# Block products of gate and value in two rounds of 15, with sums of weights and substitutions on GpSimd

## The chip, the cores and the metric

The kernel runs on one core of one Trainium2 chip. The metric is device time in microseconds of one execution; lower is better. TensorE is called PE here, VectorE DVE, ScalarE ACT, GpSimd POOL and SyncE SP, as in the profile.

## The reference

A delta-rule attention block is followed by a SwiGLU feed-forward block, all in float32:

```python
# q, k, v: (4, 8, 768, 48), beta: (4, 8, 768)
k_n = k / (norm(k, axis=-1) + 1e-06)
state = zeros((B, H, D, D))
for t in range(S):
    y[:, :, t] = einsum('bhd,bhde->bhe', q[:, :, t], state)
    v_old = einsum('bhde,bhd->bhe', state, k_n[:, :, t])
    state += beta[:, :, t] * einsum('bhd,bhe->bhde', k_n[:, :, t], v[:, :, t] - v_old)
x = y.transpose(0, 2, 1, 3).reshape(3072, 384)
g, val = x @ w_gate, x @ w_val            # (384, 1536) each
out = (g / (1 + exp(-g)) * val) @ w_out   # (1536, 384)
```

## The kernel before

The sequence is cut into 12 chunks of 64 positions, so a chunk has 256 tokens (4 batches of 64) and its x is 384 by 256: three blocks of 128 features by two blocks of 128 tokens. Two chunks form a group, and the recurrence inside a chunk is solved with a triangular inverse that is made per group.

**Attention work.** `products` turns and multiplies k and q of a chunk (`gram`). `invert(g)` makes the inverse of group g: transposes, a power on POOL (L826), scaling (`scale_m`), then `substitute`, 31 steps of two dependent DVE operations each (L593 a product into `tmp`, L599 an addition to `zb`), then transposes. `join` (for group 1 `join_late`) completes the inverse with small matmuls. `advance(c)` has four steps: the old values (L918, L927), the new ones (L957), the state and the outputs (L1025, L1013), and last the transposes of y (L1086) and the copy into the chunk's x (L1092). Group 0 is solved apart at the start.

**Feed-forward work.** Chunks 0 and 1 use plain products (`gate_val`, L1289, and `output`, L1316) while the weights arrive and are converted. From chunk 2 on (`FAST`), gate and value are made in `gate_val_fast`, three rounds per chunk. A round takes two pairs of output blocks and forms the 12 products of 3 feature blocks, 2 pairs and 2 token blocks with 11 (7 for a 2 by 2 by 2 part, 4 plain). Each of these products is `product4`: four matmuls of 128 by 128 with 128 columns (L1193), for two blocks of gate and two of value, into one PSUM bank. Sums of weight blocks are made once by DVE (`sum_of_w`, spread over `output(1, 1)` by `sums_at`), are kept in device memory (`kept`), and are loaded by SP before each use (L1220). Sums of x are four DVE operations per chunk (`sums_of_x`, L1357). ACT copies partial results between banks (L1206, L1246, L1249) and DVE adds them (L1360); ACT's Silu (L1223) and DVE's product (L1228) end each result. `output_fast` multiplies by `w_out` with 7 products for 8 (L1399), with DVE sums of h.

**Order.** All engines' queues are written out by hand in program order. Between products, `point(c)` issues one step of attention work for the next chunk and `fill(n)` hands out pieces of `invert` until about n us of DVE work are spent; a piece that yields `WAIT` ends the fill, so that work on POOL has time. `finish` issues what is left of the next chunk's steps. `load_late` issues postponed loads on SP.

Of the kernel before, what the change touches and what calls it, by code (L numbers as in the profile page):

```python
# [15 lines left out]
R = 32  # L16
# [4 lines left out]
def kernel(  # L21
# [42 lines left out]
    ffn_pool = ctx.enter_context(tc.tile_pool(name="ffn", bufs=2))  # L64
# [129 lines left out]
    wg_sb = const.tile([128, KT, DFF], FP32, name="wg_sb")  # L194
    wv_sb = const.tile([128, KT, DFF], FP32, name="wv_sb")
# [392 lines left out]
    def substitute(mb, zb):  # L588
        for j in range(R - 1):
            m = R - 1 - j  # L590
            tmp = work.tile([128, 256], FP32, name="tmp", bufs=1)
            t_v = tmp[:, 0 : (j + 1) * m].rearrange("p (k i) -> p k i", i=m)
            nc.vector.tensor_tensor(  # L593
                out=t_v,
                in0=zb[:, 0 : j + 1, j : j + 1].to_broadcast([128, j + 1, m]),
                in1=mb[:, j : j + 1, j + 1 : R].to_broadcast([128, j + 1, m]),
                op=ALU.mult,
            )
            nc.vector.tensor_tensor(  # L599
                out=zb[:, 0 : j + 1, j + 1 : R],  # L600
                in0=zb[:, 0 : j + 1, j + 1 : R],
                in1=t_v,
                op=ALU.add,
            )
            yield
# [86 lines left out]
    def first_scale(r_b):  # L692
        zb, b = first_of["zb"], beta_b[:, 0]
        nb = work.tile([128, R], FP32, name="nb", tag="nb_1", bufs=1)
# [10 lines left out]
    def first_substitution():  # L705

        zb, mb = pairs_of_blocks(first_of["zb"]), pairs_of_blocks(first_of["mb"])
        for j in range(B16 - 1):
            m = B16 - 1 - j
            shape = [128, 2, m, j + 1]  # L710
            tmp = work.tile([128, 256], FP32, name="tmp", bufs=1)
            t_v = tmp[:, 0 : 2 * (j + 1) * m].rearrange(
# [64 lines left out]
    def join_late(g, c, tags):  # L777
# [9 lines left out]
        for m in range(M):  # L787
# [5 lines left out]
        t2 = work.tile(  # L793
            [128, M, R], FP32, name="t2", tag="r" if g else "tmp", bufs=2 if g else 1
        )
# [19 lines left out]
    def invert(g):  # L815
# [26 lines left out]
        for j, _ in enumerate(substitute(mb, zb)):  # L842
            yield 1 if g == 1 else 0.4 + (j + 1) * (R - 1 - j) / 340
        if g == 1:
            yield from late_z(g, zb)
            return
        yield from turn(z_v[:, R:C], zb.rearrange("p k i -> p i k"))
# [58 lines left out]
    def advance(c):  # L906
# [169 lines left out]
        xts[c] = ffn_pool.tile([128, KT, TOK], FP32, name="x_ffn")  # L1076
# [38 lines left out]
    def w_s(n, c):  # L1115
        if n < 4:
            return units(hp[5 + n])
        return units(hp[10] if c == FAST else p_places[0][:, 0:512])

    def m5_of(c, r):  # L1120
        early = c == FAST and r == 0
        return units(hp[13] if early else p_places[0][:, 512:1024])

    kept = {
        (n, r): dram.tile([128, 4, 128], FP32, name=f"w_s{n}_{r}")
        for n in (1, 2, 4)
        for r in range(3)
    }
    x_t = const.tile([128, 3, 128], FP32, name="x_t")

    def w_pair(m, t, f):
        return (wg_sb, wv_sb)[m][:, t, 128 * f : 128 * f + 256].rearrange(
            "p (i n) -> p i n", i=2
        )

    made_in = {
        0: {1: hp[6], 2: hp[7], 4: hp[10]},
        1: {1: hp[1], 2: hp[2], 4: hp[0]},
        2: {1: hp[12], 2: hp[13], 4: hp[8]},
    }  # L1140

    def sum_of_w(n, r):

        f1, f2 = 2 * r, 2 * r + 6
        for m in range(2):
            s1, s2, s4 = (units(made_in[r][k])[:, 2 * m : 2 * m + 2] for k in (1, 2, 4))
            if n == 1:
                plus(s1, w_pair(m, 0, f2), w_pair(m, 1, f2))
            elif n == 2:
                minus(s2, s1, w_pair(m, 0, f1))  # L1150
            elif n == 4:
                minus(s4, w_pair(m, 1, f1), s2)
            else:
                minus(w_pair(m, 0, f2), w_pair(m, 0, f1), w_pair(m, 0, f2))
        if n != 3:
            nc.sync.dma_start(out=kept[n, r], in_=units(made_in[r][n]))

    sums_at = {
        2: [(1, 1), (2, 1), (4, 1)],
        4: [(1, 2), (2, 2), (4, 2)],  # L1160
        6: [(3, 1), (3, 2)],
        8: [(1, 0), (2, 0)],
        12: [(4, 0), (3, 0)],
    }

    def sums_of_w(f):
        for job in sums_at.pop(f, ()):
            sum_of_w(*job)

    def sums_of_x(c):  # L1170

        left, right = slice(0, 128), slice(128, 256)
        b1, b2 = xts[c][:, 0], xts[c][:, 1]
        minus(x_t[:, 0], b1[:, right], b1[:, left])
        minus(x_t[:, 1], b2[:, right], x_t[:, 0])
        minus(b1[:, right], b2[:, right], b1[:, right])
        minus(x_t[:, 2], b2[:, left], x_t[:, 1])
# [8 lines left out]
    ROUNDS = 3  # L1186

    p_x, p_w, p_y, p_v = (units(bank) for bank in ffn_banks)
    tok = slice(0, 128), slice(128, 256)

# [7 lines left out]
    def plain(t, f):  # L1198
        return lambda u: w_pair(u // 2, t, f)[:, u % 2]

    def summed_w(n, c):
        return lambda u: w_s(n, c)[:, u]

    def begin(c, r):
        product4(p_x, plain(0, 2 * r), xts[c][:, 0, tok[0]], True)
        nc.scalar.copy(p_y, p_x)  # L1206

    def clear(part):
        area = ffn_banks[2 + part][:, 0:DH]
        nc.scalar.copy(area, mask_q[:, 0:1].to_broadcast([128, DH]))  # L1210

    def gate_val_fast(c, r, fill):

        f1, f2 = 2 * r, 2 * r + 6
        x, m5 = xts[c], m5_of(c, r)

        def next_sums(n):
            to = c + (r == ROUNDS - 1)
            if to < NCH:
                nc.sync.dma_start(out=w_s(n, to), in_=kept[n, (r + 1) % ROUNDS])  # L1220

        def silu(p, n):
            nc.scalar.activation(  # L1223
                sil[:, n].rearrange("p (i n) -> p i n", i=2), p[:, 0:2], ACTF.Silu
            )

        def times(p, n, f, j):
            nc.vector.tensor_tensor(  # L1228
                out=h_of(c, f, j),
                in0=sil[:, n].rearrange("p (i n) -> p i n", i=2),  # L1230
                in1=p[:, 2:4],
                op=ALU.mult,
            )

        more = 1.5 if (c, r) <= (FAST + 1, 0) else 0

        def combo_and_fill(n):
            if c == FAST:
                combos.pop(0)()
                n -= 1.9  # L1240
            fill(n)

        for f in (f1, f2):
            new_h(c, f, f // 2)
        product4(p_w, summed_w(1, c), x_t[:, 0], True)
        nc.scalar.copy(m5, p_w)  # L1246
        next_sums(1)
        product4(p_y, summed_w(2, c), x_t[:, 1])
        nc.scalar.copy(p_v, p_y)  # L1249
        next_sums(2)  # L1250
        load_late()
        product4(p_x, plain(1, f1), x[:, 1, tok[0]])
        product4(p_x, plain(2, f1), x[:, 2, tok[0]])
        plus(p_y, p_y, m5)
        product4(p_v, plain(0, f2), x[:, 0, tok[1]])
        silu(p_x, 0)
        fill(1)
        times(p_x, 0, f1, 0)
        plus(p_w, p_v, m5)
        point_and_fill(c + 1, 3.4 + more, fill)  # L1260
        product4(p_y, summed_w(4, c), x[:, 1, tok[1]])
        next_sums(4)
        load_late()
        product4(p_y, plain(2, f1), x[:, 2, tok[1]])
        silu(p_y, 1)
        times(p_y, 1, f1, 1)
        product4(p_w, plain(2, f2), x[:, 2, tok[1]])
        silu(p_w, 0)
        times(p_w, 0, f2, 1)
        product4(p_v, plain(1, f2), x_t[:, 2])  # L1270
        product4(p_v, plain(2, f2), x[:, 2, tok[0]])
        silu(p_v, 1)
        sums_of_h(c, f2)
        times(p_v, 1, f2, 0)
        if r < ROUNDS - 1:
            begin(c, r + 1)
        else:
            clear(0)
        point_and_fill(c + 1, 5 + more, combo_and_fill)
# [28 lines left out]
    def output(c, bp, fill, between=()):  # L1308
        p_o = ps_ffn([128, DM], "p_o", bp)
        for f in range(FT):  # L1310
            if f in between:
                fill(2)
                point(2)
                if (c, bp) == (1, 1):
                    sums_of_w(f)
# [61 lines left out]
    def s_of(x, f):  # L1377

        t = hp[8 + f // 2].rearrange("p (x i n) -> p x i n", x=2, i=2)
        return t[:, x - 1]  # L1380

    def sums_of_h(c, f):
        f1 = f - FH
        nc.vector.tensor_tensor(
            out=s_of(1, f1), in0=h_of(c, f1, 1), in1=h_of(c, f, 1), op=ALU.add
        )
        minus(s_of(2, f1), s_of(1, f1), h_of(c, f1, 0))
        minus(h_of(c, f1, 1), h_of(c, f1, 0), h_of(c, f1, 1))

    def output_fast(c, fill):  # L1390

        p = {(1, part): ps_ffn([128, DH], "p_o", 2 + part) for part in range(2)}

        def product(x, part, a, b):
            begun = (x, part) in p
            if not begun:
                p[x, part] = ps_ffn([128, DH], "p_o", 2 * x + part)
# [16 lines left out]
        def product_2():  # L1414
            product(0, 1, lambda f: s_of(2, f), lambda f: w_t2[:, f])
# [9 lines left out]
        def product_5():  # L1425
            product(1, 1, lambda f: s_of(1, f), lambda f: w_t1[:, f])
# [373 lines left out]
```

## Time and profile before

| | |
|---|---|
| runs | 695.4, 698.79, 699.6 us; median 698.79 |
| span of the profiled execution | 694.1 us |
| PE, DVE, ACT, POOL busy | 680.5, 473.1, 259.8, 53.5 us |
| granted TensorE clock | 0.997 of full speed |
| first and last L1289 (plain gate and value) | 44.8 and 129.6 us |
| first and last L1316 (plain output) | 129.8 and 169.7 us |
| first and last L1193 (fast gate and value) | 172.1 and 676.1 us |

The profiled execution's own whole time is not listed beside its span; the span lies 1.3 us below the lowest of the runs and 4.7 us below their median. A float32 matmul of the program stands as two records in the trace. Line numbers such as L1193 are those of the kernel before; those of the changed kernel differ.

### The profile page before, as it was taken

What the parts mean: (1) busy time and instruction counts of PE and PEld (TensorE: products, weight loads), DVE (VectorE), ACT (ScalarE), POOL (GpSimd) and SP (SyncE); (2) the same over time, 40 slices, a digit from 0 to 9 for tenths busy, and PEclk for the clock granted to TensorE, in tenths of its full rate; (3) what the DMA queues carried; (4) which work ended last, traced back from release to release, by engine and by line L of the source; (5) the groups of instructions that cost most, each with busy time, mean ns of one, the idle gap of its engine ahead of it and who ended that gap; (6) DMA issues with size and microseconds to landing.
All of it is one profiled execution on the core that took longest, in us unless ns stands there. A gap on an engine that the chain in (4) does not pass through costs nothing.

```text
span 694.1 us, 25652 instructions
## 1 busy us (share of the span) xinstructions
PE 680.5 (98%) x11380; PEld 635.6 (92%) x11380; DVE 473.1 (68%) x1104; ACT 259.8 (37%) x549; POOL 53.5 (8%) x62
## 2 busy tenths in 40 slices
PE   8799999999999999999999999999999999999997
PEld 4688888757999999999999999999999999999997
DVE  6887779798899758896469786389844345333342
ACT  4674776214442532344233244242153142142230
POOL 5110031105000030000300002100000000000000
PEclk9999999999999999999999999999999999999999
DMA  9567924017550621564432363243241231221210
GB/s 136 148 167 180 275 69 161 1 34 174 133 109 16 117 79 40 103 116 84 94 72 70 73 135 70 56 108 70 55 108 48 58 83 46 55 63 46 69 47 23
DMA packets 143854, 62.31 MB, mean 90 GB/s; under 512 B 122976, under 2 KB 126048, under 8 KB 143744
## 3 DMA queue, kind: packets, MB, share of 16 engines
q1 hardware_dynamic: 141536, 60.19, 37.0%
q8 instruction: 89, 1.46, 0.9%
q10 hardware_dynamic: 2080, 0.39, 0.4%
q0 software_dynamic: 128, 0.10, 0.1%
q14 instruction: 21, 0.17, 0.1%
HBM read 53.58 MB, written 7.08 MB: 87 GB/s over the span
## 4 chain that ended last, share of the span: by engine, by line
PE 90%; DMA 4%; SPq 3%; ACT 1%; issue 1%; DVE 1%; POOL 0%; ACTq 0%; POOLq 0%; DVEq 0%
PE ffn L1193 43%; PE ffn L1399 20%; PE ffn L1289 8%; PE ffn L1316 4%; DMA h_f<-in_moe_w_val_dram 3%; PE p_px L957 2%; PE p_px L918 2%; PE p_py L1013 2%; SPq L140 1%; PE p_py L927 1%; PE p_py L521 1%; PE p_px L1025 1%; PE p_px L521 1%; SPq L186 1%; PE p_py L1086 1%; DMA wo_sb<-in_moe_w_gate_dram 1%
## 5 line engine op out<-in xcount | busy, mean ns | idle before, releaser
L1193 PE MATMUL ffn<-x_ffn,wg_sb 128*128 128x128 f32 x840 | 128.3, 275 | 0.3 <-ACT x_ffn L1092 0.2
L1193 PE MATMUL ffn<-x_ffn,wv_sb 128*128 128x128 f32 x840 | 128.1, 275 | 0.0
L1193 PEld LDWEIGHTS ffn<-x_ffn,wg_sb 128*128 128x128 f32 x840 | 111.1, 192 | 0.6 <-ACT ffn L1249 0.3
L1193 PEld LDWEIGHTS ffn<-x_ffn,wv_sb 128*128 128x128 f32 x840 | 110.7, 192 | 0.0
L1223 ACT ACTIVATE sil<-ffn 128x256 f32<-128x256 f32 x120 | 46.1, 384 | 131.8 <-PE ffn L1193 127.1
L1399 PE MATMUL ffn<-wo_sb,h_f 128*128 128x192 f32 x480 | 83.4, 327 | 0.0
L1228 DVE TENSOR_TENSOR h_f<-sil,ffn 128x256 f32<-128x256 f32 x120 | 49.5, 418 | 47.7 <-ACT sil L1223 45.2
L1399 PEld LDWEIGHTS ffn<-wo_sb,h_f 128*128 128x128 f32 x480 | 78.1, 190 | 0.4
L1360 DVE TENSOR_TENSOR ffn<-ffn,p_sb 128x512 f32<-128x512 f32 x58 | 40.4, 696 | 44.1 <-ACT ffn L1249 43.0
L1193 PE MATMUL ffn<-x_t,h_f 128*128 128x128 f32 x480 | 61.1, 280 | 0.0
L1193 PEld LDWEIGHTS ffn<-x_t,h_f 128*128 128x128 f32 x480 | 56.2, 191 | 1.4 <-ACT ffn L1206 0.2
L599 DVE TENSOR_TENSOR zb<-zb,tmp 128x31 f32<-128x31 f32 (+15 forms) x155 | 53.1, 342 | 5.3
L593 DVE TENSOR_TENSOR tmp<-zb,mb 128x31 f32<-128x31 f32 (+15 forms) x155 | 52.6, 339 | 4.0
L826 POOL TENSOR_TENSOR n_b<-mb,half 128x32 f32<-128x32 f32 x5 | 30.0, 6003 | 289.2 <-DVE mb L563 289.2
L1360 DVE TENSOR_TENSOR o_sb<-o_sb,ffn 128x192 f32<-128x192 f32 x49 | 17.2, 351 | 51.2 <-PE ffn L1399 49.1
L1206 ACT COPY ffn<-ffn 128x512 f32<-128x512 f32 x30 | 17.1, 571 | 63.5 <-PE ffn L1193 57.1
L1399 PE MATMUL ffn<-last_k,h_f 128*128 128x192 f32 x200 | 35.9, 327 | 0.0
L1289 PE MATMUL ffn<-x_ffn,wg_sb 128*128 128x256 f32 x144 | 34.4, 385 | 0.0
L1289 PE MATMUL ffn<-x_ffn,wv_sb 128*128 128x256 f32 x144 | 33.8, 382 | 0.0
L1399 PEld LDWEIGHTS ffn<-last_k,h_f 128*128 128x128 f32 x200 | 32.9, 190 | 0.0
L1289 PEld LDWEIGHTS ffn<-x_ffn,wg_sb 128*128 128x128 f32 x144 | 26.5, 190 | 4.3 <-DVE wg_sb L309 0.7
L1289 PEld LDWEIGHTS ffn<-x_ffn,wv_sb 128*128 128x128 f32 x144 | 27.0, 190 | 3.7
(302 smaller groups left out, 1064.3 us busy)
## 6 DMA issues: line engine op xcount, KB each, us to landing
h_f<-w_s SPq DMA_DIRECT2D x60, 256.0 KB, 2.9
p_sb<-w_s SPq DMA_DIRECT2D x27, 256.0 KB, 2.7
vin<-in_v_dram SPq DMA_DIRECT2D x48, 96.0 KB, 3.2
out_dram<-o_sb SPq DMA_DIRECT2D x48, 96.0 KB, 2.2
kn<-in_k_dram SPq DMA_DIRECT2D x20, 192.0 KB, 4.7
zt<-in_moe_w_out_dram SPq DMA_DIRECT2D x6, 384.0 KB, 3.7
qpad<-in_q_dram SPq DMA_DIRECT2D x36, 64.0 KB, 3.2
w_s<-h_f SPq DMA_DIRECT2D x7, 256.0 KB, 4.1
```

The source lines that it names most:

```text
L521: nc.tensor.matmul(p_v[par][half_of(b if of_q else b ^ par), bp, j], kt[c][half_of(par), bp, j, b], xt[half_of(par), bp, j, b],)
L593: nc.vector.tensor_tensor(out=t_v, in0=zb[:, 0 : j + 1, j : j + 1].to_broadcast([128, j + 1, m]), in1=mb[:, j : j + 1, j + 1 : R].to_broad ...
L599: nc.vector.tensor_tensor(out=zb[:, 0 : j + 1, j + 1 : R], in0=zb[:, 0 : j + 1, j + 1 : R], in1=t_v, op=ALU.add,)
L826: nc.gpsimd.tensor_tensor(out=n, in0=mb.rearrange("p j i -> p (j i)")[:, 0 : R * R : R + 1], in1=half, op=ALU.pow,)
L1193: nc.tensor.matmul(p[:, u], w(u), moving, start=start and u == 0, stop=True, skip_group_check=True,)
L1206: nc.scalar.copy(p_y, p_x)
L1223: nc.scalar.activation(sil[:, n].rearrange("p (i n) -> p i n", i=2), p[:, 0:2], ACTF.Silu)
L1228: nc.vector.tensor_tensor(out=h_of(c, f, j), in0=sil[:, n].rearrange("p (i n) -> p i n", i=2), in1=p[:, 2:4], op=ALU.mult,)
L1289: nc.tensor.matmul(ps[name][:, i], w_sb[:, t, (f + i) * 128 : (f + i + 1) * 128], xts[c][:, t], start=(t == 0 and i == 0), stop=(t == KT - 1),
L1316: nc.tensor.matmul(p_o, hs[c, f - f % 2][:, f % 2, bp * 128 : (bp + 1) * 128], wo_sb[:, f], start=(f == 0), stop=(f == FT - 1),)
L1360: nc.vector.tensor_tensor(out=out, in0=a, in1=b, op=ALU.add)
L1399: nc.tensor.matmul(p[x, part], a(f - f % 2)[:, f % 2], b(f), start=not begun and f == 0, stop=f == FH - 1, skip_group_check=True,)
```

## The change

From chunk 2 on, a round takes three pairs of output blocks and forms the 18 products of 3 feature blocks, 3 pairs and 2 token blocks with 15, so a chunk has two rounds of 15 instead of three of 11. Six of the 15 use sums of weights (`FORMS`), nine use x sums. The six sums of each round are made by POOL (`sums_of_w`, 15 operations of 512 elements per round), round 1's after the last `gate_val` of chunk 1 and round 0's after chunk 0's output, and POOL stores them. Loads go through a ring of four buffers. Seven partial results pass through four banks with ACT copies and DVE additions; the last result of a round is ended in the next round or in the output (`tail`). `substitute` runs on POOL for groups 2 to 5, and `fill` waits seven times for it; group 1's stays on DVE. All chunks after the first share one x buffer, and the fourth step of `advance` is held back while x is in use.

```diff
+    x_all = const.tile([128, KT, TOK], FP32, name="x_ffn")
+    tmp_of = {
+        nc.vector: x_flat[:, KT * TOK : KT * TOK + 256],
+        nc.gpsimd: hp[9][:, 256:512],
+    }
...
-    def substitute(mb, zb):
+    def substitute(mb, zb, engine=nc.vector):
         for j in range(R - 1):
...
-            nc.vector.tensor_tensor(
+            engine.tensor_tensor(
                 out=t_v,
...
-        for j, _ in enumerate(substitute(mb, zb)):
-            yield 1 if g == 1 else 0.4 + (j + 1) * (R - 1 - j) / 340
         if g == 1:
+            for _ in substitute(mb, zb):
+                yield 1
             yield from late_z(g, zb)
             return
+        for _ in substitute(mb, zb, nc.gpsimd):
+            pass
+        for _ in range(7):
+            yield WAIT
...
+    FORMS = (1, 9, 7, 6, 8, 12)
+    PAIRS = ((0, 2, 6), (8, 4, 10))
+    ring = [more_w, hp[10], hp[6], hp[7]]
...
+    def used(n, c, r):
+        if (c, r) != (FAST, 0):
+            reload(place_in_ring(c, r, n) + len(ring))
...
+    def sums_of_w(r):
+        def of(out, a, b, op=ALU.subtract):
+            nc.gpsimd.tensor_tensor(out=out, in0=a, in1=b, op=op)
+        def keep(n):
+            nc.gpsimd.dma_start(out=kept[n, r], in_=made_in[r][n])
+        of(b(1, 1), b(1, 2), b(1, 1))
+        of(w[7], b(1, 1), b(0, 1))
+        keep(7)
...
     def sums_of_x(c):
-        minus(x_t[:, 0], b1[:, right], b1[:, left])
...
+        plus(x[3], x_of(c, 0, 0), x_of(c, 0, 2))
+        plus(x[9], x[3], x_of(c, 1, 0))
+        plus(x[14], x[9], x_of(c, 1, 2))
+        minus(x[4], x[14], x_of(c, 1, 1))
+        plus(x[8], x_of(c, 0, 0), x_of(c, 1, 0))
+        minus(x_of(c, 0, 0), x_of(c, 0, 0), x_of(c, 0, 1))
+        minus(x[7], x_of(c, 0, 1), x[8])
+        plus(x[10], x[7], x_of(c, 1, 1))
+        minus(x[5], x[10], x_of(c, 1, 2))
+        minus(x[6], x_of(c, 0, 1), x[4])
...
+    def begin(c):
+        p = units(ffn_banks[parts["g"][1]])
+        multiply(p, 13, c, 0, True)
+        nc.scalar.copy(temps(c, 0)[0], p)
...
     def gate_val_fast(c, r, fill):
...
+        multiply(p4, 4, c, r, True)
+        nc.scalar.copy(p0, p4)
+        tail = parts["tail"]
+        if tail is not None:
+            tail[0]()
+            multiply(p3, 13, c, r, True)
+            multiply(p4, 3, c, r)
+            nc.scalar.copy(t0, p3)
+            multiply(p0, 1, c, r)
+            tail[1]()
+        else:
+            multiply(p4, 3, c, r)
+            multiply(p0, 1, c, r)
+        load_late()
+        multiply(p3, 2, c, r)
+        nc.scalar.copy(t1, p4)
+        plus(p1, p0, t0)
+        plus(p2, p3, t1)
+        if r > 0:
+            sums_of_h(c, 6)
+            if c == FAST:
+                combos.pop(0)()
+        point_and_fill(c + 1, 2.5, fill)
+        multiply(p0, 11, c, r)
+        multiply(p2, 9, c, r)
+        minus(t1, t1, p0)
+        multiply(p1, 7, c, r)
+        multiply(p0, 5, c, r)
+        nc.scalar.copy(t0, p1)
+        load_late()
+        multiply(p3, 0, c, r)
+        minus(p5, t0, p0)
+        finish_h(c, r, 5, p3)
+        minus(p6, t0, p2)
+        point_and_fill(c + 1, 2.5, fill)
+        multiply(p0, 6, c, r)
+        multiply(p5, 10, c, r)
+        plus(t1, t1, p0)
+        load_late()
+        multiply(p6, 8, c, r)
+        finish_h(c, r, 4, p5)
+        finish_h(c, r, 1, p0)
+        multiply(p2, 14, c, r)
...
+        def last():
+            multiply(p6, 12, c, r)
+            plus(t1, p6, t1)
...
+    def more_sums_of_h(c):
+        for f in range(0, FH, 2):
+            minus(h_of(c, f, 0), s_of(f), h_of(c, f, 0))
...
         def first_product():
+            clear(0)
             product(0, 0, lambda f: h_of(c, f, 0), quarter(0, 0))
+            end_of_rounds()
+            clear(1)
             nc.scalar.copy(o[0][:, right], p[0, 0])
+            more_sums_of_h(c)
...
     def point(c):
         mine = c < NCH and steps("advance", c) < 4 and may_advance(c)
+        if steps("advance", c) == 3 and parts["x used"]:
+            mine = False
...
         need(len(pieces))
+        sums_of_w(1)
         for bp in range(NB):
             point(2)
             output(0, bp, fill, (4, 8))
+        sums_of_w(0)
         output(1, 0, fill, (4, 8))
         hold.clear()
         first_blocks(True)
         first_blocks(False)
         point(2)
         output(1, 1, fill, range(2, FT, 2))
         finish(2)
         x_sums(2)
-        sums_of_w(12)
+        for at in range(1, len(ring)):
+            reload(at)
         for c in range(2, NCH):
```

## The prediction

> **What bounds the kernel now.** I read the page's busy shares and its chain, then the costliest groups, then busy time by stretch, and last the timelines of VectorE (DVE) and GpSimd (POOL) where the two overlap.
>
> ```profile
> span 694.1 us, 25652 instructions
> PE 680.5 (98%) x11380; PEld 635.6 (92%) x11380; DVE 473.1 (68%) x1104; ACT 259.8 (37%) x549; POOL 53.5 (8%) x62
> PE 90%; DMA 4%; SPq 3%; ACT 1%; issue 1%; DVE 1%; POOL 0%; ACTq 0%; POOLq 0%; DVEq 0%
> ...
> L1193 PE MATMUL ffn<-x_ffn,wg_sb 128*128 128x128 f32 x840 | 128.3, 275 | 0.3 <-ACT x_ffn L1092 0.2
> ...
> L599 DVE TENSOR_TENSOR zb<-zb,tmp 128x31 f32<-128x31 f32 (+15 forms) x155 | 53.1, 342 | 5.3
> L593 DVE TENSOR_TENSOR tmp<-zb,mb 128x31 f32<-128x31 f32 (+15 forms) x155 | 52.6, 339 | 4.0
> ```
>
> TensorE is the bound: busy 98%, 90% of the chain, and the block products of L1193 alone are 43% of it (the chain by line). Only removed matmuls can shorten the steady part, and anything that makes TensorE wait is paid in full. The stretches show where it might come to wait:
>
> ```profile
> 123.00:151.00 28.00, 28.00 (x157) 18.36 (x156) 23.53 (x67) 4.18 (x9) 1.99 (x3) 1.00 0.06 15
> 151.00:172.00 21.00, 20.54 (x613) 13.95 (x611) 17.95 (x38) 7.89 (x14) 9.19 (x3) 1.00 0.56 126
> 336.00:390.00 54.00, 54.00 (x1012) 52.78 (x1002) 37.68 (x89) 17.68 (x38) 6.58 (x3) 1.00 0.33 76
> ```
>
> The columns after the length are busy time of PE, PEld, DVE, ACT and POOL. In a steady chunk (third row) DVE has 16 us to spare and POOL 47. From 123 to 172 us, between the weights' conversion and the first fast chunk, DVE is busy 41 of 49 us and holds the one long dependent row, the substitution of group 1:
>
> ```profile
> 139.09 0.42 DVE L593 TENSOR_TENSOR tmp<-zb,mb 128x256 f32<-128x256 f32 x1
> 139.55 0.42 DVE L599 TENSOR_TENSOR zb<-zb,tmp 128x256 f32<-128x256 f32 x1
> ...
> 151.00 0.21 DVE L599 TENSOR_TENSOR zb<-zb,tmp 128x31 f32<-128x31 f32 x1
> 151.24 2.23 DVE L768 STREAM_TRANSPOSE zt<-zb 128x1024 f32<-128x1024 f32 x1
> ```
>
> It ends at 151.2; the join, chunk 2's state steps and x's copy follow, and the first L1193 starts at 172.1, 20.9 us later. The changed kernel leaves this row on DVE and sets POOL's 30 sums of weights beside it. What POOL and DVE do to each other is therefore the question:
>
> ```profile
> 24.06 0.31 POOL L259 COPY h_f<-h_f 128x1 uint32<-128x1 uint32 x1 [6.36 <-DMA h_f<-in_moe_w_gate_dram]
> 117.08 1.81 POOL L1631 MEMSET zt<- 128x2048 f32 x1 [16.58 <-DMA p_sb<-in_moe_w_out_dram]
> ...
> 158.89 8.04 POOL L826 TENSOR_TENSOR n_b<-mb,half 128x32 f32<-128x32 f32 x1 [33.75 <-DVE mb L563]
> ...
> 241.62 5.44 POOL L826 TENSOR_TENSOR n_b<-mb,half 128x32 f32<-128x32 f32 x1 [71.17 <-DVE mb L563]
> ```
>
> ```profile
> 24.05 0.28 DVE L723 TENSOR_TENSOR zt<-zt,tmp 128x120 f32<-128x120 f32 x1
> 24.37 0.27 DVE L717 TENSOR_TENSOR tmp<-zt,wo_sb 128x110 f32<-128x110 f32 x1
> ...
> 117.40 1.71 DVE L289 TENSOR_SCALAR staged<-wo_sb 128x384 uint32<-128x384 uint32 x1
> 119.02 0.34 DVE L289 TENSOR_SCALAR p_sb<-wo_sb 128x384 uint32<-128x384 uint32 x1
> ```
>
> POOL's one-element copy takes 0.18 us elsewhere; here 0.31, to 0.04 us after DVE's two-input operation ends. POOL's power takes 8.04 us where DVE runs two-input sums back to back, 5.44 where it does not. And DVE's 0.35 us operation takes 1.71 because POOL's memset runs until 118.9. So each shuts the other out for a whole instruction. No row has a DVE operation of two SBUF inputs beside a long POOL read.
>
> **The change, part by part.** The sum is made against the profiled execution's span, 694.1 us; the runs are 695.4 to 699.6, median 698.8, 4.7 above it, and I carry the difference over to the median.
>
> *Removed products.* 33 products per chunk become 30, for ten chunks: 30 products of 4 matmuls, two records each, 240 records. The chain gives L1193 43% of 694.1 = 298.5 us for 2640 records, 0.113 us each. **-27.1 us.** (That 1% is about what a measurement of this kernel can tell from no change: 7 us.)
>
> *A copy without cover.* In the first round of each chunk, product 4 goes into a bank, ScalarE copies the bank, and product 3 adds to the same bank with nothing between (later rounds put products 12 and 13 there). The wait: 0.275 until the last matmul ends, 0.037 to ACT's start (as L1206 behind L1193), 0.570 the copy, 0.050 back to PE, less the 0.112 after which the next would start anyway, and 0.10 because the first matmul after a wait is spaced 0.21: 0.92 us, ten times. **+9.2.**
>
> *Seven results in four banks.* DVE's PSUM sums go from 6 to 14 per chunk (L1360, 0.696 each). Products 9 and 6 need a sum that starts when the product before last ends: 0.16 + 0.04 + 0.70 + 0.05 = 0.95 against one product of 0.90, so 0.05 and 0.10 for the restart, where no state or join matmuls (1.1 us a block, L918 to L1025) stand between; and in the output the second set of h sums makes a product wait 0.35. I take 0.5 per chunk, **+5**; bounds 0.2 (all covered) and 1.2 (none).
>
> *Chunk 2's start.* POOL is free at 123.6, after the zb copy that stays where it is. Its queue is then 30 two-input sums of 512 elements, 12 DMA issues (0.55 each, L430), two memsets (0.95), group 2's power. The nearest row for a sum is L696, 0.25 for 32 elements. Bounds for the other 480: the memsets' 0.85 ns an element gives 0.66 in all; two reads at the copies' 1.87 ns (0.18 for 1, 0.24 for 32) give 2.05. I take one such read, 1.15. The Trainium skill (GPSIMD Engine Reference, Performance versus the Vector engine) has 4497 ns for a two-input add of 2048, from which 512 would be 1.1 to 1.2 as an estimate. If the engines shut each other out, POOL gets in at each of DVE's 34 ns gaps (as at 24.06) and DVE then waits out the sum. Until POOL is through, DVE does one step per sum (30) and 0.55/0.38 per issue (17), 47 of its 62, so nearly all 30 fall into the substitution; 28 x 1.15 = 32 us, less the 2.3 that DVE stood idle: it ends at 181 instead of 151.2. The eight us of sums taken from DVE lie behind it, beside PE's join, and shorten nothing. Chunk 2 then starts at 181 + 20 = 201: **+29**; 15 and 55 at the bounds. The Trainium skill (SBUF — State Buffer, Who interferes with whom) says just this: a DVE instruction with two SBUF inputs contends with a GpSimd one that reads SBUF, and the pair is locked for a whole instruction; the rows above bear out the lock, none the pairing.
>
> *Substitutions on POOL.* 62 dependent steps of 176 elements on average: 0.25 + 144 x 0.00187 + 0.08 gap = 0.60, 37 us; DVE's two-input work adds some 7. The order puts 45 to 52 us of TensorE work between first step and first reader, so it just fits; at 2.05's price (0.87 a step, 54 us) it is up to 9 late. DVE loses 85 us of work, worth nothing, since it bounded nothing. But at a chunk boundary the ten x sums (L1357, 0.28) would each wait a POOL step: about 5 us, then two transposes (1.2 each), then the first PSUM sum that product 11 waits for; after a slack of some 2, 3 us lost at three boundaries. **+9**; 0 to 16.
>
> *At nothing.* Reloads: 12 for 9 per chunk, each 2.9 us, issued at least eight products (7 us) ahead; without that cover 2.9 each. One x buffer: x is written after the last product that reads it; its copy (0.80) and the four sums needed first (1.3) lie beside two output products of 1.96; uncovered, 2 per chunk.
>
> Sum: -27.1 + 9.2 + 5 + 29 + 9 = +25, span 719, **median 724 us, slower**.
>
> **The rivals.**
> *The engines don't exclude each other in such reads* (faster). Then only POOL's queue counts: 30 x 1.15 + 12 x 0.55 = 41 us ends at 164.8, memsets 166.7, power 172.1; DVE's chain behind it (2.7 for n and mb, 0.95 for v, 1.3 for x) ends at 177, 4 later than now. -27 + 9 + 5 + 4 = -9: **690**, 684 to 696. It decides if DVE loses under 9 us in all to POOL. For it: no row shows the pairing, and DVE's 1.23 us product at 123.26 ran beside a memset unharmed (a memset reads nothing). Against: the rows at 24.06 and 158.89, and a copy at 49.04 that took 0.53 until DVE's scaling of v ended.
> *POOL is simply slow*: at 2.05 a sum, without exclusion, the queue ends at 192, power at 199, chunk 2 at 204, +31, and the substitutions come late, +6: -27 + 9 + 5 + 31 + 6 = +24, **723**. For it: no row has a POOL sum longer than 32 elements. Against it: 2.05 takes two reads at the price of the dearest row.
> *Half exclusion*: a lock held for part of a sum, or DVE served first: +10 at chunk 2, +3 later: **699**.
>
> **How the numbers follow.** Forecast 0.60 (own range 705 to 745, from the 15 and 55); no exclusion 0.24; slow POOL 0.10; half 0.06. Faster by over 1% (under 691.8) is most of the second: 0.19. Within 1%: the rest of it, most of the half case and the forecast's cheap end: 0.14. Slower: 0.67. The range 687 to 742 leaves out the fastest of the second case and the dearest of the first.
>
> **What would show it.** Right: L593's and L599's successors on DVE between 124 and 180 last 1 to 1.6 us instead of 0.42; POOL's sums of 512 start to start 1.5 us; TensorE idle some 28 us before the first product, which starts near 200; ten waits of PE on ACT of about 0.8 us; PE time between later chunks 2.7 us shorter less 1 to 2. Wrong: DVE's steps keep 0.42 beside the sums and chunk 2 starts before 180; or TensorE idle builds up inside the rounds, over 1.5 us a chunk, which would mean that the bank waits were mis-sized.

## The result and the profile after

The changed kernel takes 725.1 us (median of 4 runs, 722.5 to 727.7); the kernel before, run on the same chips, 697.1 (695.4 to 699.6). The ratio is 1.040, with a 95% interval of 1.036 to 1.044: slower by 4%. The span of the profiled execution went from 694.1 to 720.7 us, 26.6 more. These are lines of the page after: the span, the busy times, and TensorE (PE) and its granted clock in 40 slices of 18 us.

```profile
span 720.7 us, 25429 instructions
...
PE 668.6 (93%) x11140; PEld 613.7 (85%) x11140; DVE 491.8 (68%) x972; ACT 252.0 (35%) x539; POOL 229.0 (32%) x348
...
PE   8899999950999999999999999999999999999997
...
PEclk9799999995899999999999999999999999999999
```

TensorE is busy 12 us less (668.6 for 680.5) and the kernel is 27 us longer. One slice and a half holds the difference. Busy time by stretch says where (PE, PEld, DVE, ACT, POOL, then granted clock, DMA share and GB/s):

```profile
123.00:155.00 32.00, 31.89 (x169) 20.42 (x167) 30.59 (x25) 4.65 (x10) 28.77 (x27) 1.00 0.23 79
155.00:182.00 27.00, 0.56 (x42) 0.60 (x45) 25.62 (x42) 0.00 (x0) 12.88 (x13) 0.57 0.37 75
182.00:201.00 19.00, 18.66 (x584) 13.04 (x575) 9.01 (x16) 8.32 (x15) 8.26 (x5) 0.89 0.05 13
```

From 155 to 182 TensorE has nothing to do, while DVE is busy 25.6 of 27 us with 42 instructions. In the 32 us before, DVE is "busy" 30.6 us with only 25 instructions. What they are shows in the two engines' timelines, side by side (start, us, engine, line, tiles). First DVE's product ahead of the substitution of group 1 and some of its steps, then POOL's sums of weights and its issues of stores:

```profile
122.10 1.23 DVE L587 TENSOR_TENSOR mb<-mb,nb 128x1024 f32<-128x1024 f32 x1
...
146.70 1.32 DVE L599 TENSOR_TENSOR x_t<-zb,mb 128x207 f32<-128x207 f32 x1
148.06 0.37 DVE L605 TENSOR_TENSOR zb<-zb,x_t 128x207 f32<-128x207 f32 x1
148.47 2.95 DVE L599 TENSOR_TENSOR x_t<-zb,mb 128x220 f32<-128x220 f32 x1
151.46 0.39 DVE L605 TENSOR_TENSOR zb<-zb,x_t 128x220 f32<-128x220 f32 x1
...
178.91 0.21 DVE L605 TENSOR_TENSOR zb<-zb,x_t 128x31 f32<-128x31 f32 x1
```

```profile
122.15 2.30 POOL L1172 TENSOR_TENSOR w_gv<-w_gv 128x512 f32<-128x512 f32 x1
...
146.52 1.27 POOL L1172 TENSOR_TENSOR h_f<-w_gv 128x512 f32<-128x512 f32 x1
148.09 0.56 POOL L1175 DMA_DIRECT2D w_s<-h_f  x1 [0.30 <-POOL h_f L1172]
148.68 1.27 POOL L1172 TENSOR_TENSOR w_gv<-w_gv 128x512 f32<-128x512 f32 x1
149.90 1.27 POOL L1172 TENSOR_TENSOR h_f<-w_gv,h_f 128x512 f32<-128x512 f32 x1
151.46 0.56 POOL L1175 DMA_DIRECT2D w_s<-h_f  x1 [0.30 <-POOL h_f L1172]
```

Read them by their ends. DVE's step at 148.47 ends at 151.42; POOL's second sum ends at 151.17 and its queue then issues a store. DVE's next step, 0.39 us, fits into the time of that issue; a step of the same kind beside a sum lasts 1.3, beside two sums 2.95. POOL keeps its 1.27, but for the first sum: it was issued 0.05 us behind DVE's product at 122.10, which has two SBUF inputs, and took 2.30. So the one that comes second waits, whichever engine it is on. The substitution advances mostly while POOL does something other than a sum. It ends at 179.1 (before: 151.2), and the first block product starts at 200.2 (before: 172.1).

The trace has 26 of these sums, 13 a round, as the code has; the 15 operations a round in the section on the change, and the 30 sums of the prediction and of the expectations below, are miscounted. One sum lies ahead of the substitution and 25 beside it: they take 31.9 us, and DVE's 62 steps are 30.7 us longer together than in the kernel before.

From the first block product to the last the changed kernel takes 503.4 us, the kernel before 504.0, and behind the last 17.1 for 18.0. So the later start, 28.1 us, is more than the whole loss of 26.6, and with 240 matmul records fewer the steady part gained 0.6 us.

The other place is the list of what TensorE waited for (line, releaser, us in total, times, longest):

```profile
PE p_px L797 <- issue: 26.5, 1, 26.5
PE ffn L1228 <- ACT ffn L1282: 7.0, 10, 1.4
...
PE ffn L1472 <- ACT ffn L1464: 1.4, 1, 1.4
...
PE ffn L1228 <- DVE p_sb L1422: 1.0, 3, 0.6
PE ffn L1472 <- DVE h_f L1422: 0.9, 1, 0.9
```

The first row is the stretch just shown: L797 is the join, which reads what DVE transposes at the end of the substitution; the view names no releaser ("issue"), but it starts at 181.44, 0.1 us after that transpose ends. The second row is product 3 behind ScalarE's copy, ten times. Everything else is small, one by one; added up it was not.

### The profile page after: what moved, and what is told of

Read it like the earlier page. It is cut to its first block, busy times and chain, and to the rows that moved or that the text cites. A ratio compares the mean times of both kernels' runs of the same rounds, so it can differ in the third digit from the quotient of the medians.

```text
span 720.7 us, 25429 instructions
## 1 busy us (share of the span) xinstructions
PE 668.6 (93%) x11140; PEld 613.7 (85%) x11140; DVE 491.8 (68%) x972; ACT 252.0 (35%) x539; POOL 229.0 (32%) x348
## 5 line engine op out<-in xcount | busy, mean ns | idle before, releaser
L1228 PE MATMUL ffn<-x_t,w_gv 128*128 128x128 f32 x800 | 108.5, 279 | 9.6 <-ACT ffn L1282 7.0
L1228 PEld LDWEIGHTS ffn<-x_t,w_gv 128*128 128x128 f32 x800 | 97.1, 192 | 13.6 <-ACT ffn L1282 8.9
L1228 PE MATMUL ffn<-x_ffn,w_gv 128*128 128x128 f32 x640 | 86.4, 278 | 0.7 <-DVE h_f L1422 0.4
L829 POOL TENSOR_TENSOR n_b<-mb,half 128x32 f32<-128x32 f32 x5 | 28.1, 5617 | 167.3 <-DVE mb L570 167.3
L1228 PEld LDWEIGHTS ffn<-x_ffn,w_gv 128*128 128x128 f32 x640 | 78.4, 192 | 2.5 <-issue 0.6
L605 POOL TENSOR_TENSOR zb<-zb,h_f 128x31 f32<-128x31 f32 (+15 forms) x124 | 72.5, 585 | 9.7
L599 POOL TENSOR_TENSOR h_f<-zb,mb 128x31 f32<-128x31 f32 (+15 forms) x124 | 64.5, 520 | 14.4 <-DVE mb L587 5.0
L1422 DVE TENSOR_TENSOR ffn<-p_sb,ffn 128x512 f32<-128x512 f32 x38 | 26.4, 696 | 35.8 <-PE ffn L1228 35.2
L1425 DVE TENSOR_TENSOR o_sb<-o_sb,ffn 128x192 f32<-128x192 f32 x49 | 17.1, 348 | 29.9 <-PE ffn L1472 24.4
L1356 PE MATMUL ffn<-x_t,w_gv 128*128 128x256 f32 x144 | 34.4, 387 | 0.1
L1356 PE MATMUL ffn<-x_ffn,w_gv 128*128 128x256 f32 x144 | 31.7, 380 | 0.0
L1309 ACT COPY p_sb<-ffn 128x512 f32<-128x512 f32 x19 | 11.1, 585 | 57.8 <-PE ffn L1228 57.8
L1381 PE MATMUL ffn<-wo_sb,h_f 128*128 128x384 f32 x88 | 31.1, 508 | 0.0
```

Source lines behind the costliest of these rows:

```text
L599: engine.tensor_tensor(out=t_v, in0=zb[:, 0 : j + 1, j : j + 1].to_broadcast([128, j + 1, m]), in1=mb[:, j : j + 1, j + 1 : R].to_broadcas ...
L605: engine.tensor_tensor(out=zb[:, 0 : j + 1, j + 1 : R], in0=zb[:, 0 : j + 1, j + 1 : R], in1=t_v, op=ALU.add,)
L829: nc.gpsimd.tensor_tensor(out=n, in0=mb.rearrange("p j i -> p (j i)")[:, 0 : R * R : R + 1], in1=half, op=ALU.pow,)
L1228: nc.tensor.matmul(p[:, u], w(u), moving, start=start and u == 0, stop=True, skip_group_check=True,)
L1309: nc.scalar.copy(t0, p1)
L1356: nc.tensor.matmul(ps[name][:, i], w_sb[:, t, (f + i) * 128 : (f + i + 1) * 128], xts[c][:, t], start=(t == 0 and i == 0), stop=(t == KT - 1),
```

## The experiments

**Each pair of operations by itself.** A small kernel of 24 stages, in which DVE and POOL each run a row of one operation:

```
for d, g in stages:              # go and done tie the two queues at each stage's ends
    for _ in range(pool[g]): g() # sum, copy or memset of 512 elements, or a DMA issue
    for _ in range(dve[d]): d()  # 256 elements: two SBUF inputs, one SBUF and one PSUM, ...
```

> This kernel leaves out the whole computation (it stores zeros) and measures the disputed price by itself: in 24 short stages, each begun together, VectorE (DVE) runs a row of 256-element fp32 operations of one kind (sum of two SBUF inputs; sum of one SBUF and one PSUM input; scale by a constant; copy; 32x32 transpose) and GpSimd (POOL) a row of 512-element operations of one kind (sum of two inputs, copy, memset; in the last stage DMA issues), after stages with each engine alone. Theory of the prediction (each shuts the other out for a whole instruction when DVE has two SBUF inputs and POOL reads SBUF): DVE's two-SBUF sum, 0.42 us alone, takes 1.3 us or more beside POOL's sums (about one per sum), also beside POOL's copies, and 0.42 beside memsets; DVE's sum with a PSUM input keeps its time alone beside everything; POOL's sum takes 1.27 alone and the same beside DVE. Rival, any SBUF access of POOL counts: DVE's sum is as late beside memsets as beside sums. Rival, POOL is slow only because DVE disturbs it (shared rate instead of a lock): POOL's sum alone takes clearly under 1.27, about 0.7, and DVE's steps are all lengthened a little instead of some by a whole POOL instruction. DVE's scale and copy: the row at 117.40 of the kernel before (1.71 us beside a memset) lets expect that a memset holds them up; the transpose is open.

Busy time by stretch, here of DVE and of POOL (the two small copies that tie the queues are among them). In order: POOL's sums alone; DVE's sum of two SBUF inputs alone; the same beside POOL's sums, copies and memsets; DVE's sum with a PSUM input beside POOL's sums; DVE's scaling by a constant beside sums and beside memsets; DVE's transpose beside sums.

```profile
2.30:10.60 8.30, 0.00 (x0) 7.79 (x8) 1.00 0.00 0
25.80:34.90 9.10, 8.45 (x22) 0.71 (x2) 1.00 0.00 0
70.10:85.00 14.90, 14.25 (x22) 8.56 (x8) 1.00 0.00 0
85.10:96.60 11.50, 10.85 (x21) 6.07 (x10) 1.00 0.00 0
96.70:105.90 9.20, 8.55 (x22) 8.26 (x17) 1.00 0.00 1
106.10:115.00 8.90, 8.25 (x21) 7.86 (x8) 1.00 0.00 0
133.40:148.60 15.20, 14.28 (x29) 7.90 (x8) 1.00 0.00 0
160.70:174.00 13.30, 12.38 (x29) 8.60 (x17) 1.00 0.00 0
214.80:223.20 8.40, 7.24 (x18) 7.81 (x8) 1.00 0.00 1
```

The 20 sums of DVE take 9.1 us alone, 14.9 beside six sums of POOL, 11.5 beside copies, 9.2 beside memsets. With one input in PSUM they take 8.9 beside sums: no difference. POOL's sum takes 1.26 alone and 1.31 beside DVE's. So for DVE's sums it is a lock of two SBUF reads on DVE against a read on POOL, not POOL being slow (the second rival) and not any access (the first). Of the 8.3 us beside POOL's sums DVE lost 5.8, POOL 0.3. DVE's scaling, with one input, is shut out too, by sums (28 in 15.2 us instead of 9.2) and by memsets (13.3); a transpose is not. The Trainium skill (SBUF — State Buffer, Who interferes with whom) has the same pairs: two SBUF inputs on DVE contend with a GpSimd instruction that reads SBUF and not with one that only writes it, and DVE's copies and scalings, in their two-port modes, contend with GpSimd too. The runs agree. On who blocks, that section says that the order of issue decides. In these rows it was DVE that lost, and in the kernel POOL where DVE's product came first.

**The reads taken out, the queue kept.** In place of each of the 26 sums, `nc.gpsimd.memset(out, 0.02)` twice, and once on half of it.

> The changed kernel with each of POOL's 30 weight sums replaced by three memsets of the same place (512, 512 and 256 elements, about 1.3 us together), so the sums of weights are left out; issues, queue and order stay. Theory of the prediction (POOL's reads shut out DVE's steps of two SBUF inputs): the substitution of group 1 runs at 0.42 us a step again and ends near 151 to 153, the first block product starts at 172 to 175, span 693 to 697, median 697 to 701. Rival, POOL's queue is simply too long: the queue is as long as before, so chunk 2 starts near 200 still, 722 to 727. Rival, any SBUF access of POOL locks: 720 to 727.

709.4 us, ratio to before 1.017 (1.014 to 1.020): between the two forecasts. DVE beside the memsets, and what TensorE waited for most:

```profile
139.36 0.42 DVE L599 TENSOR_TENSOR x_t<-zb,mb 128x247 f32<-128x247 f32 x1
139.81 0.42 DVE L605 TENSOR_TENSOR zb<-zb,x_t 128x247 f32<-128x247 f32 x1
...
154.26 2.23 DVE L773 STREAM_TRANSPOSE zt<-zb 128x1024 f32<-128x1024 f32 x1
```

```profile
PE ffn L1230 <- DVE x_t L1424: 9.7, 1, 9.7
PE ffn L1230 <- ACT ffn L1284: 7.8, 11, 1.4
```

The lock is gone, and the first product starts at 175.2. Then product 4 waits 9.7 us: POOL gets to group 2's power only at 174.7, DVE's steps behind the power stand in its queue ahead of the x sums, and product 4 needs four of these. That is the wait of my "no exclusion" rival (chain behind the power), which the lock had covered. It is longer than the 4 us given there, since the memsets and issues take 48 us (124.7 to 172.9) where I had counted 41 for sums and issues.

**The same with the sums in place.** The accumulator of group 1 goes to PSUM:

```
+            z_p = ps_pair("z_p", "py").rearrange("p e n -> p (e n)")
+            z_p = z_p.rearrange("p (k i) -> p k i", i=R)
+            nc.scalar.copy(z_p, zb)
-            for _ in substitute(mb, zb):
+            for _ in substitute(mb, z_p):
...
-            yield from late_z(g, zb)
+            yield from late_z(g, z_p)
```

> The changed kernel with one difference: the accumulator zb of group 1's substitution stands in PSUM (ScalarE copies POOL's initial zb there, 1.1 us), so that each of DVE's 62 steps has one SBUF input instead of two; all 30 sums stay on POOL at the same place. Theory (the lock needs two SBUF inputs on DVE; in the run of pairs the sum with a PSUM input kept 0.42 beside everything): steps of 0.42 or less, the substitution ends at 151 to 154, the first product starts at 172 to 175; then the queue of POOL is next, as in the run with memsets: sums to 167, power to 174.5, DVE's x sums behind what the power releases, so 5 to 9 us of waiting before product 4: median 701 to 708. Rival (the queue or the number of DVE steps sets chunk 2's start, not the lock): 722 to 728.

706.8 us (704.9 to 708.6), ratio 1.013 (1.010 to 1.016).

```profile
139.24 0.42 DVE L599 TENSOR_TENSOR x_t<-p_py,mb 128x247 f32<-128x247 f32 x1
139.69 0.42 DVE L605 TENSOR_TENSOR p_py<-p_py,x_t 128x247 f32<-128x247 f32 x1
```

```profile
PE ffn L1231 <- DVE x_t L1425: 6.5, 1, 6.5
```

Same engines, same sums, same queue; only where one operand stands has changed, and the steps are 0.42 again. The substitution ends at 154.2, and 6.5 us remain of the wait for the power. This settles that the lock held chunk 2 back.

**The power ahead of the last sums.** As above, and the last sums are issued after group 2's power. Of the 13 sums and 6 stores of the round, `slice(0, 11)` takes 7 sums and 4 stores and leaves 6 sums and 2 stores, not the 8 and 7 sums of the expectation:

```
-        sums_of_w(0)
+        sums_of_w(0, slice(0, 11))      # 7 sums, 4 stores
...
+        if g == 2:                      # in invert, right after the power
+            sums_of_w(0, slice(11, None))
```

> The kernel with zb in PSUM, and POOL's second set of sums cut in two: the first 8 sums and 3 stores where they were, then group 2's power, then the last 7 sums. Theory (with the lock gone, only the power's place in POOL's queue keeps chunk 2 back): power at 158 to 164, x sums as in the kernel before, no wait of TensorE over 1 us before the first four products; all of the 28 us are back, median 695 to 699. Rival (the last sums, at 165 to 176, come late for products 6, 8 and 12 of the first round, or the substitution of group 2 comes late for chunk 4): 700 to 708.

702.1 us, ratio 1.006 (1.004 to 1.008): outside what I expected, inside the rival's range, but not by the rival's mechanism, since no wait of TensorE in the trace is put down to a sum of weights. TensorE still waits 2.7 us before product 4:

```profile
PE ffn L1237 <- POOL h_f L599: 2.7, 1, 2.7
```

The view names POOL there; product 4 reads an x sum of DVE, which stands behind DVE's product for group 2. The run with all three edits, below, shows why that is late.

**Together with the new order of the first round.** First the order alone, in the changed kernel:

```
             multiply(p4, 4, c, r, True)
             nc.scalar.copy(p0, p4)
-            multiply(p4, 3, c, r)
+            multiply(p3, 2, c, r)
             multiply(p0, 1, c, r)
+            multiply(p4, 3, c, r)
...                                      # then 11, 7, 9 for 11, 9, 7
```

> The changed kernel with another order of products in the first round of each chunk: 4, 2, 1, 3, 11, 7, 9 for 4, 3, 1, 2, 11, 9, 7, so that ScalarE's copy of product 4 runs beside product 2 (the sums take the same operands). The trace after has ten waits of 0.82 us beyond the ordinary step there (0.66 idle and 0.10 restart). Theory (the copy without cover costs 0.92 each, 9.2 us in all, and nothing else is behind it): 8 to 9 us faster, 716 to 718. Rival (the wait moves on: the first PSUM sum or product 9 then waits for DVE): 0 to 4 us faster, 721 to 725.

718.2 us (717.9 to 718.4), 7.0 under the changed kernel: between the two forecasts, near the first. The wait on line L1282 went from 7.0 us in ten to 0.9 in two:

```profile
PE ffn L1228 <- ACT ffn L1282: 0.9, 2, 0.5
```

Then all three:

> All three together: zb in PSUM, the sums cut in two around the power, and the order 4, 2, 1, 3, 11, 7, 9 in each chunk's first round. If the terms add up (28 for chunk 2's start, 7.0 as measured for the order): 725.1 - 28 - 7 = 690, 687 to 692, about 1% under the kernel before. Rival (chunk 2's first round, which now runs beside POOL's last sums, needs the cover elsewhere): 693 to 700.

693.7 us, ratio 0.995 (0.993 to 0.997), 1.7 above what I gave and inside the rival's range. TensorE waits 3.1 us before product 4 of chunk 2. DVE's row ahead of the x sums has this step in it:

```profile
173.00 2.78 DVE L587 TENSOR_TENSOR mb<-mb,nb 128x1024 f32<-128x1024 f32 x1
```

In the kernel before:

```profile
170.33 1.23 DVE L580 TENSOR_TENSOR mb<-mb,nb 128x1024 f32<-128x1024 f32 x1
```

It has two SBUF inputs, and POOL's last sums run at that time: the same lock, moved to group 2.

**The last sums on DVE.** With all three edits, `sums_of_w(0, slice(11, None), nc.vector)` after the power, the stores still on POOL.

> The kernel with all three edits, and the last 7 sums (after group 2's power) on DVE instead of POOL, in the stretch from 158 to 170 in which DVE stood idle for 9.6 us. In the run before, TensorE waited 3.1 us before product 4 of chunk 2: DVE's product for group 2 (L587, two SBUF inputs) took 2.78 us instead of 1.23, and two smaller steps 0.5 more each, beside POOL's last sums. Theory (that is the same lock, and it is the last of it): the wait goes down to about 0.5, median 690 to 692. Rival (DVE's 5 us of sums hold up its subtraction for v, which waits in the same queue, or lock against the power): 693 to 697.

```profile
173.38 1.23 DVE L587 TENSOR_TENSOR mb<-mb,nb 128x1024 f32<-128x1024 f32 x1
```

689.9 us (689.4 to 693.6), ratio 0.988 (0.986 to 0.991): 1.2% faster than the kernel before and 4.9% faster than the changed one. The wait before product 4 is 0.6 us.

**All sums on DVE** (the part of the change undone: `nc.vector` for `nc.gpsimd` in `of`).

> The changed kernel with the 30 sums of weights on DVE instead of POOL, at the same place in the order (stores still issued by POOL). Theory (the lock costs 28 us; on DVE the sums cost their own time): 30 sums of 0.69 to 0.75 are 21 to 22 us in the same queue as the substitution, less the 4.5 that DVE stood idle there: the substitution ends at 168 to 171 instead of 179, the first product at 189 to 192: median 713 to 718. Rival (DVE has the room, as it made 8 us of sums in the kernel before without delay): 698 to 706.

712.9 us (710.0 to 713.2), ratio 1.021 (1.018 to 1.023). A sum takes 0.69 there and the 26 take 17 us, not the 21 to 22 of the expectation; the substitution ends at 169.4, the first product starts at 190.5. Undoing this part gives back 12 us, where the PSUM operand and the power's place give back 23 (725.1 to 702.1): 17 us of work in the row that sets the start put it off by 18 us, the lock by 28.

**Later substitutions back on DVE** (with the kernel before's weights for spreading them over the fills).

> The changed kernel with the substitutions of groups 2 to 5 on DVE as in the kernel before (spread over the fills), the rest as changed. By the prediction's sum (9 us lost at chunk boundaries by POOL's steps shutting out DVE's x sums): 714 to 719. By the trace after, in which I find only about 3 us of TensorE's waiting that POOL's steps could have caused (0.6 before product 4 of chunk 2, 1.4 in chunk 3, 0.8 at the join): 719 to 724. Rival, DVE has no room for them now that it has 14 PSUM sums and 10 x sums a chunk (85 us of steps more, about 10 a chunk): its sums come late for the products, 726 to 735.

811.0 us, ratio 1.163 (1.158 to 1.167): 86 us slower than the changed kernel, far outside everything that I had written, on the side of the rival. Page lines, then TensorE's waits:

```profile
PE 699.5 (86%) x11140; PEld 639.6 (79%) x11140; DVE 561.2 (69%) x1220; ACT 253.0 (31%) x539; POOL 92.6 (11%) x100
...
PEclk9799999958999999899999599999699999679999
```

```profile
PE ffn L1470 <- DVE h_f L1420: 10.1, 7, 2.9
PE ffn L1226 <- DVE p_sb L1420: 9.7, 9, 1.6
...
PE ffn L1470 <- DVE h_f L1260: 5.2, 4, 1.9
PE ffn L1226 <- DVE h_f L1260: 5.0, 4, 1.4
PE ffn L1226 <- DVE ffn L1423: 4.6, 7, 1.1
```

DVE is busy 69%, hardly more than before. But a bundle of substitution steps now stands in its queue ahead of sums that the next product needs: at 409.6 us, for one, six steps of 2.3 us stand ahead of the sum that runs from 411.9 to 412.6, and TensorE waits 1.6 us for it. TensorE's idle time summed over the trace is 104 us for 46 in the changed kernel, and its 11140 matmuls are busy 31 us longer at a lower granted clock: 58 and 31 make the difference. Whether another placing of the steps would do better was not tried; this is the price of this one.

**Later substitutions left out.**

> The changed kernel with the 248 steps of POOL's substitutions of groups 2 to 5 left out (POOL's 37 us a group). The prediction put 9 us on them (x sums held up by the lock at three chunk boundaries, late readers): then 714 to 718. The trace of the changed kernel shows DVE's x sums lengthened from 0.28 to 0.6 there, but only some 0.6 to 2.5 us of TensorE's waiting at places that they could explain: then 721 to 725.

722.7 us (720.7 to 724.3), ratio 1.034 (1.030 to 1.037): 2.5 us under the changed kernel, whose runs go from 722.5 to 727.7, so less than that spread, and far from 9; in the profiled executions the time from the first to the last block product is 501.3 for 503.4 us.

**DVE's sums left out.** The six `plus` and `minus` between products in each round, and those of h.

> The changed kernel with DVE's sums between the products left out: the six sums with a PSUM input in each round, and the sums of h between the output's products (the products themselves stay, their inputs then are whatever the places hold). What TensorE loses by waiting for them is the prediction's 0.5 us a chunk for seven results in four banks, 5 us in all, bounds 2 to 12: then 719 to 721. By the trace after, in which I add up 4.1 us of waits between products, some 2 of restarts behind them and 4.3 more in the output's products than before: 713 to 716.

709.6 us, ratio 1.016 (1.014 to 1.019): 15.5 under, more than either forecast gave. From first to last block product 491.3 us for 503.4, that is 12.1 less; the rest lies in the stretches before and behind, where executions of one kernel also scatter by some us. Both are above my 5.

## Why the prediction was right, and where it was not

The forecast was 724 us and the time 725.1, by the forecast's mechanism. The change itself was given as +25 and came out as +26.6 by the spans and +28.0 by the medians, since the median before was 697.1 in these runs and not 698.8. That it is so near is in part luck, as the terms show:

| term | predicted | measured |
| --- | --- | --- |
| removed products | -27.1 | -26.9 (240 at the ordinary step of 0.112) |
| copy without cover | +9.2 | +9 to 10 in the steps of the trace; 7.0 by the new order |
| seven results in four banks | +5 (2 to 12) | +12.1 by the run, +11.1 by the trace |
| chunk 2's start | +29 | +28.1 |
| substitutions on POOL | +9 (0 to 16) | +2.1, near the spread |
| sum | +25 | about +25, of 26.6 |

*Chunk 2's start* came out by its mechanism: POOL's sum 1.27 (taken: 1.15), 1.2 to 1.4 us from sum to sum without an issue (said: 1.5), end of the substitution at 179.1 (said: 181), 21.1 us from there to the first product (said: 20). But its size rests on two errors that cancelled: 28 sums beside the substitution at 1.15, 32.2 us, were 25 at 1.27, 31.9 us. With the measured price and 28 sums the term would have been 3.4 us dearer, with 25 sums at 1.15 3.4 us cheaper. The detail was off too: I had DVE gain one step after each sum. POOL often had its next sum going before DVE came in, so steps of 2.95 beside two sums and 5.3 us beside four stand in the row and others at 0.4, through POOL's issues. By the end of POOL's last store, at 167, DVE had begun 30 of its 62 steps, where I had given 47. The total is nearly the same, because nearly all of POOL's sums were locked time; the last 12 us of the substitution ran beside two memsets and then alone.

*Seven results in four banks* was mis-sized: near its dear bound. In the changed kernel's trace, steps between products that are longer than 0.112 add up to 4.1 us (apart from the copy and from product 4's x sums), the slower first step after a wait to another 2.7, and the output's products take 141.8 us for 137.5. So the output was nearly right, 4.3 us where I had 0.35 a chunk; the rounds, which I had at 0.15 a chunk, took 0.7, in many small waits of which hardly one is over 1 us. I had said that over 1.5 us a chunk would prove me wrong; it was 1.2. The other sign, that the time from chunk to chunk falls by 2.7 less 1 to 2, so by 0.7 to 1.7 us, failed narrowly: from the end of chunk 2's output to the end of the last it fell from 463.6 to 459.2 us, 0.5 a chunk.

*Substitutions on POOL* was mis-sized the other way. DVE's x sums do stretch, from 0.28 to about 0.6, but TensorE reaches the products that need them later than that. My slack at the boundaries was too small. The two errors, +7 and -7, cancelled; the median would have been as good with neither, but it is luck that both were not on one side.

*"DVE loses 85 us of work, worth nothing, since it bounded nothing"* was true of the kernel before and wrong for the changed one. There DVE must deliver 14 PSUM sums a chunk on time, and with the substitutions in its queue, spread as before, the time is 811. The move to POOL does not speed anything up; against that placing it keeps the 15 products from losing far more than they save.

The rivals: *no exclusion* fell with the first timeline, and its conditional wait (the chain behind the power) turned up as the next in line once the lock was gone, with 6.5 us. *POOL is simply slow* fell with 1.27 us, and *half exclusion* with 30.7 us of stretched steps beside 31.9 us of sums. The granted clock of 0.972, which I had not foreseen, is mostly the idle stretch itself (0.57 there, 0.89 after): it costs nothing visible, since the 21 us from substitution to first product are what they were.

## What to carry to other kernels

Before moving elementwise work to POOL, list what DVE does at that time: in these runs operations with two SBUF inputs stopped for as long as POOL read, and the busy row of DVE then shows stretched steps rather than idle time. If the lock falls on a row that sets a start, one operand in PSUM removed it here for the price of a copy of 1.0 us; then look what stands next in POOL's own queue. An engine with a low share can still be the one whose order decides: ask what the next consumer waits for behind each moved piece, in the changed kernel and not in the old one.

## What the hardware showed that I had not expected

- The lock is lopsided: with both rows back to back, DVE lost 5.8 us of 8.3, POOL 0.3. Where DVE's longer product came first, POOL's sum lost 1.0 (2.30 for 1.27).
- One operand in PSUM costs DVE's sum nothing: 20 sums of 256 elements take 8.9 us beside POOL with it, 9.1 without it alone.
- POOL's DMA issues (0.56 us each) leave DVE's two-input sums alone: 0.425 us each beside four issues, as without them.
- The granted clock can fall without a long gap. In the run with the substitutions on DVE it was 0.50 between 447 and 460 us, where TensorE was busy 9.6 of 13 us and no gap was over 1.7 us. The Trainium skill (TensorE: Matmul & The Clock Gate, HAM oscillation — how this bites in real kernels) gives as its abstract rule no idle gaps over some 3.4 us. In this stretch, which holds mostly matmuls of 48 to 64 rows and columns, shorter gaps went with the low clock; no run here parts the gaps from the small matmuls.
